# A decode-step kernel: the output sum in four column tiles of one PSUM bank instead of two row groups in two banks

## Chip, core and metric

One core of one Trainium2 chip runs one launch of the kernel. The metric is the device time of a launch in microseconds (us); smaller is better. Beside the timed runs there is one profiled execution, whose trace lists every instruction of the five engines (PE, the TensorE matmul unit, with its weight loads PEld; DVE, the VectorE; ACT, the ScalarE; POOL, the GpSimd; SP, the SyncE, which here only issues transfers) and every transfer.

## The reference

A normalised input of four tokens (one per batch row, D = 576) goes through an attention over the last 2,048 positions of a key and value cache, and through an MLP mixer; both results and the input are summed.

```python
def reference(A_x, A_k_cache, A_v_cache, A_wq, A_wo, B_x, B_w1, B_w2, B_w3, B_w4):
    def _A_ref(x, k_cache, v_cache, wq, wo):          # B=4, Hq=32, Hkv=16, Sk=8192, Dh=128, W=2048
        q = (x @ wq).reshape(B, Sq, Hq, Dh).transpose(0, 2, 1, 3)
        k = jnp.repeat(k_cache[:, :, Sk - W:, :], rep, axis=1)
        v = jnp.repeat(v_cache[:, :, Sk - W:, :], rep, axis=1)
        scores = jnp.einsum("bhqd,bhkd->bhqk", q, k) * (Dh ** -0.5)
        o = jnp.einsum("bhqk,bhkd->bhqd", _softmax(scores, axis=-1), v)
        return o.transpose(0, 2, 1, 3).reshape(B, Sq, Hq * Dh) @ wo
    def _B_ref(x, w1, w2, w3, w4):                    # D=576, F=4608
        ...
        x1 = x + hs
        return x1 + _gelu(_layernorm(x1, axis=-1) @ w3) @ w4
    x = A_x
    xn = _layernorm(x, axis=-1)
    return x + _A_ref(xn, A_k_cache, A_v_cache, A_wq, A_wo) + _B_ref(xn, B_w1, B_w2, B_w3, B_w4)
```

With a sequence of one token the shifted groups that make `hs` are all zero, so `x1` is `xn`, and `w1` and `w2` are not read. What is left to read is two caches of 33.6 MB each and the weights `wq`, `wo`, `w3`, `w4`: 87.17 MB in all.

## The kernel before

**Loads.** All large loads are issued by SP, in program order, into one SBUF tile, `ring` (L113), whose regions are used again and again. An issue waits on SP until the instructions that read the region's former content are done. The order is: `wq` and `w3` (L151 to L153), the key cache in pairs and single tiles of 4 MB (`cache_load`, L126), the first half of `w4` (L509), the value cache in eight tiles, V0 to V7, and at the end 14 rows of the second half of `w4` (L562, `end[0]`), `wo` in two pieces of 23 and 9 rows of 576 columns (L565), and the remaining 3 and 1 rows of `w4` (`end[1]` and `end[2]`).

**Stages.** A prologue normalises the input, makes the transposed copies and runs the first MLP product (L248) and the query product (L267). The key stage turns each key tile with DVE transposes (L321) and multiplies (L330, sixteen times four matmuls of 512 columns in four column tiles for every tile). Then come the exponentials, and the value stage: DVE spreads the probabilities (L402), PE multiplies them by the value tiles (L415). From L516 to L578 the order of PE, ACT and DVE is written out by hand (`tc.manual_schedule`); before that the framework orders the instructions of an engine.

**The output sum.** All products that end in the output, 68 rows in all, are summed in PSUM without being copied out: 36 rows of `w4` (`mlp_out`, L495, with the columns of `gT`, the MLP's activations) and 32 rows of `wo` (L575, with the columns of `onx`, the attention's heads). `acc_matmuls` (L466) takes a weight operand of 4 columns (the four batches) and a row of 576 columns, and issues two matmuls of 288 columns each: the left half goes to partitions 0 to 3 of the bank `ACC`, the right half to partitions 32 to 35 of a second bank `ACC2`. `ACC` is opened early by a matmul with zeros (L215), and the residual `xn + x` is written into it by two DVE copies (L232). `ACC2` is opened inside the value stage after the third value tile (L545 to L547): a matmul with zeros, and a DVE copy of the right half's residual.

**The end.** After V7 the last heads are picked (L441, L439, L449, L454, L458), in between run rows of `w4`; five matmuls with zeros (`idle`, L572) keep PE working; then PE does the 32 rows of `wo` and the rows of `end[1]` and `end[2]`. DVE copies the left half to `fin`, ACT the right half (L582, 4 partitions x 288 each), and ACT issues one output transfer of 4 rows of 1,152 bytes (L583).

Of the kernel before, what the change touches and what calls it, by code (L numbers as in the profile page):

```python
# [11 lines left out]
BF16 = mybir.dt.bfloat16  # L12
F32 = mybir.dt.float32
# [5 lines left out]
def kernel(  # L19
# [19 lines left out]
    nc = tc.nc  # L39
    P = 128  # L40
    B, Sq, D = A_x.shape
# [13 lines left out]
    NF = F // P  # L55
    NFH = NF // 2
    NQ = Hq * Dh
    DC = (D // 2, D // 2)
    NI = 4
    NI1 = NFH - NI * NI  # L60
    NG2 = (NI + 1) * P
# [6 lines left out]
    o2 = out.flatten_outer_dims()  # L68

    def ap_of(t, offset_elems, dims):  # L70
        a = t[:]
        return bass.AP(a.tensor, a.offset + offset_elems, [list(a.ap[0])] + [list(d) for d in dims])
# [10 lines left out]
    const = ctx.enter_context(tc.tile_pool(name="const", bufs=1))  # L83
    small = ctx.enter_context(tc.tile_pool(name="small", bufs=2))
# [4 lines left out]
    ps_s = ctx.enter_context(tc.tile_pool(name="ps_s", bufs=4, space=PSUM))  # L89
# [19 lines left out]
    REST = 4 * TILE  # L109
    RING = max(SLOT[2] + wq_n + w3_n, REST + E0_N)  # L110
    assert wo_n + sum(E1) * D <= 2 * TILE
    LEAD = 16
    ring = ringp.tile([P, LEAD + RING], BF16, tag="ring", name="ring")[:, LEAD:LEAD + RING]  # L113

    def load_run(t, src):
# [28 lines left out]
    XR = wo_n // D  # L144
    NT = Hq * Dh // (P * XR)
# [12 lines left out]
    ident = const.tile([P, P], BF16)  # L158
# [22 lines left out]
    def z_part(n, dt):  # L181
        a = z_at[0]
        z_at[0] += n * (1 if dt is BF16 else 2)
        assert z_at[0] <= ZN
        return Z[:, a:a + n] if dt is BF16 else Zf[:, a // 2:a // 2 + n]
# [10 lines left out]
    def turned(src, count, name):  # L196
        tp = ps_tp.tile([P, count, B], BF16, tag="tp", name=name)
        for k in range(count):
            nc.tensor.transpose(out=tp[:, k, :], in_=src(k), identity=ident[0:B, 0:B])  # L199
        return tp  # L200
# [3 lines left out]
    xn_f, xn_bf, ln2_bf = (z_part(D, dt)[0:B] for dt in (F32, BF16, BF16))  # L204
# [6 lines left out]
    ACC = ps_acc.tile([P, 512], F32)  # L211

    zeros = const.tile([P, 512], BF16)
    nc.vector.memset(zeros[:], 0.0)
    nc.tensor.matmul(out=ACC[:], lhsT=ident[:], rhs=zeros[:], start=True, stop=False, skip_group_check=True)  # L215
    gT = const.tile([P, NF, B], BF16)


    QN = 512
# [8 lines left out]
    l_dup = half_rows(ln2_bf, 0, NS, NO)  # L228
    ln2T = const.tile([P, 2 * NO, B], BF16)
    nc.vector.tensor_tensor(out=xn_f[:], in0=xn_f[:], in1=x_bf[:], op=ALU.add)  # L230
    for q in range(2):
        nc.vector.tensor_copy(out=ACC[32 * q:32 * q + B, 0:DC[q]], in_=xn_f[:, q * DC[0]:q * DC[0] + DC[q]])  # L232
    tpl = turned(lambda k: l_dup[:, k % 2, NO - 1 - k // 2, :], 2 * NO, "tpl")
    nc.vector.tensor_copy(out=ln2T[:], in_=tpl[:])

# [26 lines left out]
    for j in range(-1, KJ):  # L262
        for h in range(2 if j >= 0 else 1):
            k = 2 * j + 1 - h if j >= 0 else 2 * KJ + 1
            for i in range(QI):
                f0 = (j * NQ + WT if j >= 0 else 0) + h * WT + i * QN
                nc.tensor.matmul(out=qp[32 * i:32 * i + 2 * B, :], lhsT=xnT[:, k:k + 2, :].rearrange("p e b -> p (e b)"),  # L267
                                 rhs=wq_t[:, f0:f0 + QN], start=False, stop=False, skip_group_check=True)
# [13 lines left out]
    for y in range(NY):  # L282
        for m in range(HB):
            m2, r = divmod(m, rep)
            nc.tensor.matmul(out=tq[:, :, :, m2, y, r, :],
                             lhsT=q_rows[:, m, y, :, :].rearrange("p g i -> p (g i)"), rhs=rows,
                             start=(y + m == 0), stop=(y == NY - 1 and m == HB - 1), skip_group_check=True)
# [13 lines left out]
    S = []  # L301
# [44 lines left out]
    for g0 in range(2):  # L346
        for mh in range(2):
            nc.gpsimd.tensor_copy(out=ap_of(perm_rows, 16 * g0 + 8 * mh, [[32, B], [2, 4], [1, rep]]),
                                  in_=ap_of(ident, 8 * g0 + 16 * mh, [[rep, B], [32, 4], [1, rep]]))
# [4 lines left out]
                   in_=ap_of(perm_rows, 0, [[PB, 2], [1, rep], [rep, MT]]))  # L354
# [74 lines left out]
                             start=True, stop=True, skip_group_check=True)  # L429
        nc.scalar.copy(out=rd_rows[:], in_=RD[:])  # L430

    onx = const.tile([P, NT, XR, B], BF16)

    def heads_out(bp):
        for j in range(2):
# [17 lines left out]
    def heads_pick(bp, OX):  # L453
        nc.vector.tensor_tensor(out=masked.rearrange("p t b x e -> p (t b) x e"),  # L454
                                in0=OX[:].rearrange("p t b (e x) -> p (t b) x e", x=XR),
                                in1=ap_of(own_d, 0, [[0, NT * 2], [0, XR], [1, ND]]), op=ALU.mult)
        with nc.allow_low_precision(reason="one term of each sum is not zero"):
            nc.vector.tensor_reduce(out=ap_of(onx, 2 * bp, [[XR * B, NT], [1, 2], [B, XR]]),  # L458
                                    in_=masked, op=ALU.add, axis=AX.X)

    ACCS = [ACC]

    def acc_rows(q):
        return slice(32 * q, 32 * q + B)

    def acc_matmuls(lhsT, row):  # L466
        for q in range(2):
            nc.tensor.matmul(out=ACCS[q][acc_rows(q), 0:DC[q]], lhsT=lhsT, rhs=row[:, q * DC[0]:q * DC[0] + DC[q]],  # L468
                             start=False, stop=False, skip_group_check=True)

    def gelu_u():
        nc.vector.scalar_tensor_tensor(out=gu, in0=gx[:], scalar=GA, in1=gx[:], op0=ALU.mult, op1=ALU.mult)
# [3 lines left out]
    def gelu_g():  # L476
        nc.vector.scalar_tensor_tensor(out=gg[:], in0=gu, scalar=1.0, in1=gx[:], op0=ALU.add, op1=ALU.mult)

    def gelu_T():
        GT = ps_tp.tile([P, NF, B], F32, tag="tp", name="GT")  # L480
        for i in range(NI + 1):
            n = NI if i < NI else NI1
            c_step = NI if i < NI else 1
            cols = bass.AP(ident[:].tensor, ident[:].offset, [list(ident[:].ap[0]), [32, n], [B, 2], [1, B]])
            out = ap_of(GT, (i if i < NI else NI * NI) * B, [[c_step * B, n], [NFH * B, 2], [1, B]])
            nc.tensor.matmul(out=out, lhsT=gg[:, i * P:(i + 1) * P], rhs=cols, start=(i == 0), stop=(i == NI),
                             skip_group_check=True)
        nc.scalar.mul(out=gT[:], in_=GT[:], mul=0.5)  # L488

    def load_w4(a, e, i0, n):  # L490
        t = ring[:, a:a + n * D]
# [2 lines left out]

    def mlp_out(t, e, i0, n, a=0, b=None):  # L495
        for i in range(a, n if b is None else b):
            acc_matmuls(gT[:, e * NFH + i0 + i, :], t[:, i, :])


    for n in range(len(K_order)):  # L500
# [16 lines left out]
    with tc.manual_schedule(engines=ENGINES):  # L517
        exponentials(0)
        first = ps_s.tile([P, rep, CK], F32, tag="S", name="first")
        for r in range(rep):  # L520
            pick_rows(0, r, first[:, r, :], 0, 1)
        exponentials(1)
        exponentials(2)
        for r in range(rep):
            nc.scalar.copy(out=CB[:, 0, 0, :, r], in_=first[:, r, :])
        exponentials(3)
        spread_rows(0)
        v_compute(0, 0, CK // 2)
        pick_all(0)
        keep_rows(0, 1, NG)  # L530
        v_compute(0, CK // 2, CK)
        cache_load(v_rows, 4, 1, V_tiles)
        spread_rows(1)
        reciprocals()
        nc.scalar.copy(out=spread, in_=bass.AP(fold[:].tensor, fold[:].offset, [list(fold[:].ap[0]), [1, PB], [0, ND]]))
        for n in range(1, NV):
            if n + 1 < NV:
                spread_rows(n + 1)
            v_compute(n)
            if n == 1:  # L540
                pick_all(1)
                keep_rows(1, 0, NG)
            if n == 2:
                reciprocal_rows()
                ACCS.append(ps_s.tile([P, 512], F32, tag="S", name="ACC2"))  # L545
                nc.tensor.matmul(out=ACCS[1][:], lhsT=ident[:], rhs=zeros[:], start=True, stop=False, skip_group_check=True)  # L546
                nc.vector.tensor_copy(out=ACCS[1][acc_rows(1), 0:DC[1]], in_=ACC[acc_rows(1), 0:DC[1]])  # L547
            if n == 3:
                heads_out(0)
            if n == 4:  # L550
                heads_pick(0, heads_rows(0))
                gelu_u()
            if n == 6:
                gelu_g()
                gelu_T()
                mlp_out(*w4_e0, 0, NFH // 2)
            if n + 4 < NV:
                cache_load(v_rows, n + 4, 1, V_tiles)
            if n == 5:
                wo_t, end, i0 = ring[:, 0:wo_n], [], 0  # L560
                for k, n1 in enumerate(E1):
                    end.append(load_w4(wo_n + i0 * D, 1, i0, n1))  # L562
                    i0 += n1
                    for a, b in ((0, XF * D), (XF * D, wo_n)) if k == 0 else ():
                        load_run(wo_t[:, a:b], flat(A_wo, wo_n)[:, a:b])  # L565
        heads_out(1)
        mlp_out(*w4_e0, NFH // 2, NFH * 2 // 3)
        OX = heads_rows(1)
        mlp_out(*w4_e0, NFH * 2 // 3, NFH)
        heads_pick(1, OX)  # L570
        mlp_out(*end[0])
        idle = ps_s.tile([P, 512], F32, tag="S", name="idle")  # L572
        for i in range(5):
            nc.tensor.matmul(out=idle[:], lhsT=ident[:], rhs=zeros[:], start=(i == 0), stop=(i == 4), skip_group_check=True)
        for x in range(XR):  # L575
            acc_matmuls(onx[:, 0, x, :], wo_t[:, x * D:(x + 1) * D])
        for part in end[1:]:
            mlp_out(*part)  # L578

    fin = const.tile([B, D], out.dtype, name="fin")  # L580
    for q, copy in enumerate((nc.vector.tensor_copy, nc.scalar.copy)):
        copy(out=fin[:, q * DC[0]:q * DC[0] + DC[q]], in_=ACCS[q][acc_rows(q), 0:DC[q]])  # L582
    nc.scalar.dma_start(out=o2, in_=fin[:])  # L583


# [28 lines left out]
```

## Time and profile before

| | |
|---|---|
| median of 3 runs | 210.72 us (210.34 to 210.96) |
| the profiled execution's own time | 210.92 us |
| its span, first to last instruction | 209.1 us |
| mean granted PE clock | 0.755 of full speed |
| busy: PE, DVE, ACT, POOL | 122.2, 128.0, 13.2, 4.3 us |
| PE matmuls, with as many weight loads | 1077 |

The span is what the trace shows; the rest of the execution's 210.92 us, 1.8 us, lies around it. Durations below are those of this one execution, to be held against its own time.

How the rows are read: a row of a timeline is "start, duration, engine, line, operation, written tile <- read tiles, shape, count, and in brackets the idle time of the engine before it and what ended that". An overlapping run of like instructions is merged into one row. A row of the stretches view gives for each engine the busy time and the number of instructions, the granted clock, and the share of time in which the core's 16 DMA engines were busy (a transfer is counted where it began, so a stretch can read a little over 1).

### The profile page before, as it was taken

The page shows a single profiled execution, that of the slowest core. Times are in us where ns is not written, and L with a number is a line of the kernel's source. Part 1 is how long each engine was busy: PE and PEld are TensorE (multiplying, and loading weights), DVE is VectorE, ACT ScalarE, POOL GpSimd, SP SyncE. Part 2 cuts the span into 40 slices and gives each one's busy share as a digit, 9 for nine tenths or more (in the row PEclk, how much of TensorE's full clock was granted, in tenths as well). Part 3 has the DMA queues.
Part 4 walks back from the last instruction along what each step waited for, and adds up shares of the span by engine and source line. Part 5 has one row for each costly group of instructions (what it writes and reads, how often), then busy time and mean ns, then how long its engine had stood idle before and what let it go on. Part 6 is the DMA issues. An engine that isn't in the chain of part 4 may idle for free.

```text
span 209.1 us, 2429 instructions
## 1 busy us (share of the span) xinstructions
PE 122.2 (58%) x1077; PEld 76.3 (36%) x1077; DVE 128.0 (61%) x120; ACT 13.2 (6%) x34; POOL 4.3 (2%) x15
## 2 busy tenths in 40 slices
PE   1318951001543333454333341999999999999994
PEld 0101211000111101111111110678788889878652
DVE  5930021009996999999999937139946578940200
ACT  2000022000000000000000023020210001000000
POOL 2500000000000000000000000000000000000000
PEclk9999997555555555555555555599999999999999
DMA  8989999999997999999999999999799999999991
GB/s 339 397 381 489 514 392 401 414 401 501 476 414 307 476 426 393 432 464 407 427 543 422 404 414 426 401 539 404 338 464 429 407 451 442 401 425 439 446 384 68
DMA packets 3057, 87.31 MB, mean 417 GB/s; under 512 B 348, under 2 KB 488, under 8 KB 744
## 3 DMA queue, kind: packets, MB, share of 16 engines
q1 hardware_dynamic: 3024, 87.16, 97.1%
q8 instruction: 8, 0.13, 0.2%
q10 hardware_dynamic: 24, 0.01, 0.0%
q14 instruction: 1, 0.01, 0.0%
HBM read 87.17 MB, written 0.00 MB: 417 GB/s over the span
## 4 chain that ended last, share of the span: by engine, by line
DMA 26%; PE 23%; DVE 7%; SPq 0%; issue 0%; DVEq 0%
PE O L415 20%; DMA ring<-in_A_v_cache_dram 14%; DMA ring<-in_A_wo_dram 13%; DVE kt L321 6%; PE C L379 2%; PE ACC L468 1%; DVE mx L305 0%; PE OX L449 0%; DVE fin L582 0%; SPq L116 0%; PE RD L428 0%; SPq L492 0%; PE ACC L546 0%; DVEq L321 0%
## 5 line engine op out<-in xcount | busy, mean ns | idle before, releaser
L321 DVE STREAM_TRANSPOSE kt<-ring 128x2048 int32<-128x2048 int32 x32 | 70.7, 2275 | 14.7 <-DMA ring<-in_A_k_cache_dram 14.7
L330 PE MATMUL S<-kt,Z 128*32 128x512 bf16 x256 | 30.4, 622 | 60.3 <-DVE kt L321 60.3
L415 PE MATMUL O<-ring,X 128*128 128x256 bf16 x512 | 59.5, 280 | 4.9 <-DMA ring<-in_A_v_cache_dram 4.8
L415 PEld LDWEIGHTS <-X 128*128 128x128 bf16 x512 | 51.3, 100 | 13.0 <-issue 3.0
L402 DVE TENSOR_TENSOR X<-Z,own 128x1024 int32<-128x1024 int32 x32 | 37.0, 1217 | 11.2 <-ACT Z L389 8.2
L330 PEld LDWEIGHTS <-Z 128*32 128x32 bf16 x256 | 9.9, 127 | 80.0 <-issue 74.7
L248 PE MATMUL G<-ring,ln2T 128*8 128x512 bf16 (+1 forms) x54 | 10.5, 862 | 3.9 <-DMA ring<-in_B_w_dram 3.9
L278 DVE CAST q_rows<-qp 128x256 bf16<-128x256 f32 x4 | 1.5, 418 | 16.7 <-PE qp L267 16.0
L439 DVE TENSOR_SCALAR Z<-O,rd_rows 64x128 f32<-64x128 f32 x2 | 0.7, 357 | 13.5 <-ACT Z L441 13.5
L371 ACT ACTIVATE Z<-S,nb 128x512 bf16<-128x512 f32 x4 | 2.8, 702 | 89.9 <-DVE nb L514 89.9
L248 PEld LDWEIGHTS <-ln2T 128*8 128x8 bf16 x54 | 2.0, 98 | 11.3 <-issue 9.9
L582 DVE CAST fin<-ACC 4x288 bf16<-4x288 f32 x1 | 0.4, 446 | 7.9 <-PE ACC L468 7.9
L468 PE MATMUL ACC<-ring,gT 128*4 128x288 bf16 x72 | 5.1, 286 | 0.4 <-ACT gT L488 0.4
L468 PE MATMUL ACC<-ring,onx 128*4 128x288 bf16 x64 | 4.3, 286 | 0.3 <-DMA ring<-in_A_wo_dram 0.2
L389 ACT CAST Z<-C 128x384 bf16<-128x384 f32 (+1 forms) x4 | 2.7, 663 | 21.6 <-PE C L379 21.5
L379 PEld LDWEIGHTS <-pick 128*128 128x128 bf16 x24 | 2.4, 111 | 4.3 <-issue 2.8
L199 PEld LDWEIGHTS <-Z 4*128 4x128 bf16 x16 | 0.7, 104 | 8.8 <-DVE Z L174 5.0
L305 DVE TENSOR_REDUCE mx<-S 128x1 f32<-128x512 f32 x4 | 2.7, 671 | 2.0 <-PE S L330 2.0
L379 PE MATMUL C<-Z,pick 128*128 128x512 bf16 x16 | 3.8, 379 | 0.0
L468 PEld LDWEIGHTS <-gT 128*4 128x4 bf16 x72 | 3.0, 84 | 1.8 <-ACT gT L488 0.5
L468 PEld LDWEIGHTS <-onx 128*4 128x4 bf16 x64 | 2.9, 84 | 1.9 <-issue 1.0
L547 DVE COPY ACC<-ACC 4x288 f32<-4x288 f32 x1 | 0.5, 462 | 4.7 <-PE ACC L546 4.7
(81 smaller groups left out, 46.7 us busy)
## 6 DMA issues: line engine op xcount, KB each, us to landing
ring<-in_A_k_cache_dram SPq DMA_DIRECT2D x4, 4096.0 KB, 20.5
ring<-in_A_v_cache_dram SPq DMA_DIRECT2D x4, 4096.0 KB, 20.3
ring<-in_B_w_dram SPq DMA_DIRECT2D x1, 5184.0 KB, 15.5
ring<-in_A_wq_dram SPq DMA_DIRECT2D x1, 4096.0 KB, 24.7
ring<-in_A_wo_dram SPq DMA_DIRECT2D x1, 3312.0 KB, 23.6
ring<-in_B_w_dram SPq DMA_DIRECT2D x1, 2592.0 KB, 26.9
ring<-in_B_w_dram SPq DMA_DIRECT2D x1, 2016.0 KB
ring<-in_A_wo_dram SPq DMA_DIRECT2D x1, 1296.0 KB, 26.3
```

Of the source, the lines that this page charges most:

```text
L199: nc.tensor.transpose(out=tp[:, k, :], in_=src(k), identity=ident[0:B, 0:B])
L248: nc.tensor.matmul(out=G_banks[k][32 * c:32 * c + 2 * B, 0:n * P].rearrange("p (i m) -> p i m", m=P), lhsT=ln2T[:, NS - 1 - s:NS + 1 - s, ...
L278: nc.vector.tensor_copy(out=dst, in_=src)
L305: nc.vector.reduce_max(out=mx[:, g:g + 1], in_=S[g][:], axis=AX.X)
L321: nc.vector.transpose(out=ap32(kt[e], c0 * 2 * G, [[2 * G, C2 // 2], [1, 2], [2, G]]), in_=ap32(kn, c0 * 4 * G + e * G, [[4 * G, C2 // 2], ...
L330: nc.tensor.matmul(out=S[kq][c:c + 32, :].rearrange("p (c q l) -> p c q l", q=4, l=2), lhsT=qz[:, bp, m, y, :], rhs=kt[e][:, :, 4 * m:4 * ...
L371: nc.scalar.activation(out=EP[:, g].rearrange("p q (c l) -> p c q l", l=2), in_=S[g][:].rearrange("p (c q l) -> p c q l", q=4, l=2), func= ...
L379: nc.tensor.matmul(out=out, lhsT=pick[:, bp, r, 3 - q:3 - q + P], rhs=EP[:, g0:g1, q, :], start=(q == 0), stop=(q == 3), skip_group_check= ...
L389: nc.scalar.copy(out=CB[:, bp, g0:g1, :, r], in_=CPS[bp, r][:, g0 * CK:g1 * CK].rearrange("p (g c) -> p g c", c=CK))
L402: nc.vector.tensor_tensor(out=ap32(X, a * CX * MT, [[MT, CX], [1, MT]]), in0=bass.AP(s32.tensor, s32.offset, [list(s32.ap[0]), [1, CX], [0 ...
L415: nc.tensor.matmul(out=O_tiles[bp][:], lhsT=X[:, c:c + 2, :].rearrange("p c n -> p (c n)"), rhs=vn[:, c:c + 2, :].rearrange("p c d -> p (c ...
L468: nc.tensor.matmul(out=ACCS[q][acc_rows(q), 0:DC[q]], lhsT=lhsT, rhs=row[:, q * DC[0]:q * DC[0] + DC[q]], start=False, stop=False, skip_gr ...
```

## The change

The sum lies in one bank, in four column tiles: columns 144q to 144q+143 of the output lie on partitions 32q to 32q+31 of `ACC`, columns 0 to 143. Within a tile the four batches lie eight partitions apart (0, 8, 16, 24). Each row is four matmuls of 144 columns with a weight operand of 25 columns. For that `gT` and `onx` hold the four batches of row i at the columns 5i, 5i+8, 5i+16, 5i+24, in zeroed tiles; the 25 columns from 5i on also hold values of other rows, at places that are no multiple of 8, whose products land on partitions that nobody reads. The residual comes in by four fp32 matmuls with a small operand `place` instead of by DVE copies. `ACC2`, its zero matmul and its DVE copy are gone. At the end one ACT copy takes all 128 partitions x 144 to `fin`, and the output transfer takes every eighth partition: 16 rows of 288 bytes. `LEAD` is changed by 352 bytes per partition.

```diff
-    DC = (D // 2, D // 2)
+    DQ = 4
+    DW = D // DQ
+    BS = 32 // B
+    LS = 5
+    LW = BS * (B - 1) + 1
...
-    LEAD = 16
+    LEAD = 192
...
-    gT = const.tile([P, NF, B], BF16)
+    gT = const.tile([P, LS * (NF - 1) + LW], BF16)
+    nc.gpsimd.memset(gT[:], 0.0)
...
-    for q in range(2):
-        nc.vector.tensor_copy(out=ACC[32 * q:32 * q + B, 0:DC[q]], in_=xn_f[:, q * DC[0]:q * DC[0] + DC[q]])
+    place = small.tile([B, LW], F32, tag="place")
+    nc.gpsimd.memset(place[:], 0.0)
+    nc.gpsimd.tensor_copy(out=place[:, 0:LW:BS], in_=ident[0:B, 0:B])
+
+    def acc_matmuls(lhsT, row):
+        for q in range(DQ):
+            nc.tensor.matmul(out=ACC[32 * q:32 * q + LW, 0:DW], lhsT=lhsT, rhs=row[:, q * DW:(q + 1) * DW],
+                             start=False, stop=False, skip_group_check=True)
+
+    acc_matmuls(place[:], xn_f)
...
-    onx = const.tile([P, NT, XR, B], BF16)
+    onx = const.tile([P, LS * (XR - 1) + LW], BF16)
+    nc.gpsimd.memset(onx[:], 0.0)
...
-            nc.vector.tensor_reduce(out=ap_of(onx, 2 * bp, [[XR * B, NT], [1, 2], [B, XR]]),
+            nc.vector.tensor_reduce(out=ap_of(onx, 2 * bp * BS, [[0, NT], [BS, 2], [LS, XR]]),
...
-    def acc_matmuls(lhsT, row):
-        for q in range(2):
-            nc.tensor.matmul(out=ACCS[q][acc_rows(q), 0:DC[q]], lhsT=lhsT, rhs=row[:, q * DC[0]:q * DC[0] + DC[q]],
-                             start=False, stop=False, skip_group_check=True)
+    def row_cols(t, i):
+        return t[:, LS * i:LS * i + LW]
...
-        nc.scalar.mul(out=gT[:], in_=GT[:], mul=0.5)
+        nc.scalar.mul(out=ap_of(gT, 0, [[LS, NF], [BS, B]]), in_=GT[:], mul=0.5)
...
-            acc_matmuls(gT[:, e * NFH + i0 + i, :], t[:, i, :])
+            acc_matmuls(row_cols(gT, e * NFH + i0 + i), t[:, i, :])
...
-                ACCS.append(ps_s.tile([P, 512], F32, tag="S", name="ACC2"))
-                nc.tensor.matmul(out=ACCS[1][:], lhsT=ident[:], rhs=zeros[:], start=True, stop=False, skip_group_check=True)
-                nc.vector.tensor_copy(out=ACCS[1][acc_rows(1), 0:DC[1]], in_=ACC[acc_rows(1), 0:DC[1]])
...
-            acc_matmuls(onx[:, 0, x, :], wo_t[:, x * D:(x + 1) * D])
+            acc_matmuls(row_cols(onx, x), wo_t[:, x * D:(x + 1) * D])
...
-    fin = const.tile([B, D], out.dtype, name="fin")
-    for q, copy in enumerate((nc.vector.tensor_copy, nc.scalar.copy)):
-        copy(out=fin[:, q * DC[0]:q * DC[0] + DC[q]], in_=ACCS[q][acc_rows(q), 0:DC[q]])
-    nc.scalar.dma_start(out=o2, in_=fin[:])
+    fin = const.tile([P, DW], out.dtype, name="fin")
+    nc.scalar.copy(out=fin[:], in_=ACC[:, 0:DW])
+    step = fin[:].ap[0][0]
+    nc.scalar.dma_start(out=o2.rearrange("b (q c) -> q b c", q=DQ),
+                        in_=bass.AP(fin[:].tensor, fin[:].offset, [[BS * step, DQ * B], [1, DW]]))
```

## The prediction, made before the changed kernel was run

> **What bounds the kernel now.** I read the page first, then the same span by stretches, then the issue and landing of the last loads, then the last three microseconds instruction by instruction.
>
> ```profile
> span 209.1 us, 2429 instructions
> PE 122.2 (58%) x1077; PEld 76.3 (36%) x1077; DVE 128.0 (61%) x120; ACT 13.2 (6%) x34; POOL 4.3 (2%) x15
> HBM read 87.17 MB, written 0.00 MB: 417 GB/s over the span
> ```
>
> No engine is busy for two thirds of the span, while 417 GB/s are read over all of it. The stretches show whether the transfers ever pause:
>
> ```profile
> 50.00:100.00 50.00, 20.87 (x176) 6.76 (x176) 48.17 (x23) 0.00 (x0) 0.00 (x0) 0.50 0.98 419
> 100.00:150.00 50.00, 29.56 (x228) 18.90 (x228) 36.70 (x30) 4.57 (x13) 0.00 (x0) 0.64 1.00 432
> 150.00:204.00 54.00, 52.90 (x517) 44.39 (x516) 27.53 (x30) 3.65 (x8) 0.00 (x0) 1.00 0.99 426
> ```
>
> The columns are stretch, length, busy us of PE, PEld, DVE, ACT and POOL, PE clock, DMA share, GB/s. The last two hardly move: the 16 DMA engines are full from the first load to 204, whichever engine is busy beside them. So the loads set the time, and the engines matter in two ways only: if one kept a buffer so long that the queue ran dry, or in what is left after the last load has landed. The first does not happen: a value tile takes 20.3 us from issue to landing where 4 MB at 426 GB/s take 9.8, so about ten microseconds of transfers lie queued at each issue. For the second, the last three loads:
>
> ```profile
> 178.84 0.90 SPq L492 DMA_DIRECT2D ring<-in_B_w_dram  x2
> ...
> ring<-in_B_w_dram SPq DMA_DIRECT2D x1, 432.0 KB, 26.9
> ring<-in_B_w_dram SPq DMA_DIRECT2D x1, 144.0 KB, 26.8
> ```
>
> The two issues at 178.84 and 179.31 (the pair ends at 179.74, the second takes 0.43) are end[1] and end[2], the last four rows of the sum; with 26.9 and 26.8 us to landing they arrive at 205.74 and 206.11. The 9 rows before them arrive with wo's second piece: PE waits for it until 204.72, by the chain of waits, which ends "DMA wo 26.32 from 178.37, PE ACC 1.80 from 204.72, DVE fin 0.43". And now PE and the end:
>
> ```profile
> 205.82 0.66 PE L468 MATMUL ACC<-ring,gT 128*4 128x288 bf16 x8
> 206.15 0.08 PEld L468 LDWEIGHTS <-gT 128*4 128x4 bf16 x1
> 206.51 0.45 DVE L582 CAST fin<-ACC 4x288 bf16<-4x288 f32 x1 [7.93 <-PE ACC L468]
> 206.55 0.39 ACT L582 CAST fin<-ACC 4x288 bf16<-4x288 f32 x1 [10.04 <-PE ACC L468]
> 207.04 0.27 ACTq L583 DMA_DIRECT2D out_dram<-fin  x1
> ```
>
> The reader is to see the second row: the very last weight load began at 206.15, 0.04 after the landing at 206.11, because it stood behind the matmul that waited for the load. The last two matmuls began at 206.20, 122 ns after the pair before (288 columns at 2.4 per ns are 120). So the chain of waits names PE for the last 1.80 us, but PE is late by only 206.20 - 206.15 = 0.05 us; behind that stands the last load. This is what I choose to build on.
>
> **The change part by part.**
>
> *Row pace.* Two matmuls of 288 columns in two column tiles run together: a row takes 122 ns (64 in 4.38 us with one stop). Four of 144 in four tiles would take 61 if they also run together, as the sixteen of L330 do (four of 512 columns in about 427 ns at clock 0.50). They need eight PE instructions per row instead of four. The nearest row for an issue limit is L285: 16 matmuls of 32 columns with 128-column weights in 0.64 us, 25 ns apart in a run; four one after another would be 100 ns a row. It does not matter which: PE must do 12 rows between 204.72 and 206.15, so any pace up to 1.43 / 12 = 119 ns is covered by the last load. The 23 rows of wo's first piece have 204.72 - 201.61 = 3.11 us, 135 ns each. The 0.73 us that 12 rows win at 61 ns become waiting, in front of 204.72, 205.74 and 206.11. Gain: 0.05 us. If the cover were gone it would be 0.05 + 0.7.
>
> *Last matmul.* It ends 0.286 after its start now; 144 columns fewer take 0.06 less. With the four starting together (L330's starts lie within 0.03), the sum ends at 206.15 + 0.01 + 0.23 = 206.39 instead of 206.48, a gain of 0.09 with the 0.05 in it. PE will stand idle more: between 201.15 and 204.57 the 23 rows take 1.4 us instead of 3.2. The granted clock fell to 0.50 at 33.9 us after 3.4 us with 0.64 busy, and did not after 3.4 us with 1.86 busy; 1.4 lies between, nearer to the second. If it falls, the last rows take about 122 ns again and the last matmul some 0.08 more: the gain of 0.09 is gone, no more. I take no fall.
>
> *Copy.* ACT began 0.065 after the matmul's end, took 0.389, DVE ended at 206.96, and the transfer was issued 0.08 later. One ACT copy of 128x144 from PSUM: gT at L488 has just this shape and took 0.290 (128x128 at L257: 0.272). So 206.39 + 0.065 + 0.29 + 0.08 = 206.83 for the issue, against 207.04: 0.21 gained, the 0.09 included.
>
> *Output transfer.* From its issue at 207.04 to SP seeing it landed were 1.29 us, then 0.8 to the span's end. Four packets of 1,152 bytes become 16 of 288; no row of the trace shows such a write. From below: the four landings lay 0.14 apart, which more parallel sources could remove, -0.14. From above: issues of 128 rows took 0.42 to 0.54 against 0.27, +0.26, and sixteen packets in one line at the 29 ns of x_bf's 576-byte ones are 0.46 against the 0.18 that the four take, +0.28; together +0.54. Sixteen rows are far nearer to 4 than to 128, and x_bf's short packets ran side by side: I take +0.05.
> The Trainium skill speaks against the change here: "DMA: Bandwidth & Descriptors", Specifications, puts the smallest transfer for full rate at 512 B, below which the engine reads, modifies and writes. No run here shows such a write yet; with that page's 0.2 us for an access to HBM, an estimate, the transfer would be 0.2 longer and the time 210.7.
>
> *Moved or removed elsewhere.* The four fp32 `place` matmuls and the POOL work (memsets of gT, onx and place, one copy; POOL is busy 4.3 us in all) fall into the prologue, where the first product waits 3.9 us for w3 (G at L248 <- DMA 3.9); PE's transposes queue behind `place`, but DVE loses two copies of 0.45 there. If that cover were gone, it would still lie ahead of the full queue. The ACC2 matmul (0.38) and copy (0.46) at 158.3 leave the value stage, and the 9 rows at 187.57 shrink from 1.27 us to 0.6 to 0.9; but V7 starts at 188.96 on its own landing, so both become waiting there. gT and onx are written with a stride at the same element count: nothing. LEAD makes up for smaller tiles ahead of the ring: nothing.
>
> Sum: -0.21 + 0.05 = -0.16, which I round to -0.2: the profiled execution's span goes from 209.1 to 208.9 and its time, with the 1.8 us around the span unchanged, from 210.92 to 210.7. The median of the runs shown lies 0.20 below that execution, so the forecast for it is **210.5 us**.
>
> **Rivals.**
>
> *PE pays per matmul (slower).* In L468 each matmul costs 61 ns; if that were a price per matmul and not per column, a row would take 244. Then from 197.59 on: 20 rows 4.88, idle 1.08, 36 rows 8.78, to 212.33; the last ends about 212.5 instead of 206.48, less 0.12 for the copy: +5.9, 216.6 us. It decides from 119 ns a row, a price of 30 ns per matmul. For it: 61 in L468 and 109 in L415 are the only long runs. Against it: L285's 25 ns, though these 16 had waited 2.80 us and lay ready, and 120 ns of columns explain the 122. The Trainium skill, "TensorE: Matmul & The Clock Gate", section "Wait — 56ns, not 53.3ns?", knows such a price: about 62 ns per matmul when the sequencer's firmware decodes, none with hardware decoding. The L285 row agrees with the second.
>
> *Instruction loads in the way of the data.* PE's program grows by some 280 instructions, and the instruction queue brought eight packets, 0.13 MB, for PE's 2,154: one or two more. Each puts one of 16 DMA engines behind: at 206.1 the 16 landings of the last load, one for each engine, spread over 1.76 us in the trace's records, seven at the front, eight within 0.26 of the end. One more on a fresh engine joins the late half and costs nothing; on one that is already late it would cost up to 0.9 to 1.6: 211.4 to 212.1.
>
> *A slow output.* More than the bound above: it needs some +0.85 to be seen, 211.4. For it only the short writes; against it that even 0.46 in one line does not reach that.
>
> *The last loads come sooner (faster).* If landings at 205.74 and 206.11 were late for a reason that the change removes, PE's 0.73 would count: -0.16 - 0.7 = 209.8. Against it: 87 MB at full rate, the same bytes in the same order.
>
> **Chances.** A measurement of this kernel can tell about 0.3%, 0.63 us, from no change (the three runs spread that far). The forecast, clock falling or not and output within its bounds: 0.64, between 210.1 and 211.0, all of it within 0.3%, but for a part of 0.04 that the runs' spread puts below 210.1. Sooner loads 0.12. PE's price 0.07, instruction loads 0.10, slow output 0.07; of the instruction loads some 0.03 stays within 0.3%. So faster 0.16, same 0.63, slower 0.21. The range for 8 in 10 goes from 209.8, the sooner loads, to 211.4, the lower end of the instruction loads; outside lie PE's price and the tails.
>
> **What would show it.** Right: rows of four L468 matmuls 61 to 100 ns apart, PE idle before the wo pieces and before the last row, the last matmul starting at the last landing, a copy of 0.29, the span shorter by the copy alone. Wrong: four matmuls of a row starting one after another and no PE idle before 206; the last landing moved from 206.1; the clock at 0.50 in the last rows; more than 1.9 us from the output's issue to its landing.

## The result, and the profile after

| | before | after |
|---|---|---|
| median of 5 runs each | 210.72 us (210.34 to 210.96) | 212.22 us (212.02 to 212.40) |
| ratio | | 1.0073 (95% interval 1.0058 to 1.0087) |
| the profiled execution's time, its span | 210.92, 209.1 us | 212.22, 210.4 us |

The changed kernel is slower by 1.5 us. It lies outside the forecast's range; the two profiled spans differ by 1.3. The page of the changed kernel, its heads and the instruction queue:

```profile
span 210.4 us, 2716 instructions
PE 118.3 (56%) x1220; PEld 74.7 (35%) x1220; DVE 126.8 (60%) x116; ACT 13.6 (6%) x34; POOL 5.1 (2%) x19
q8 instruction: 9, 0.15, 0.2%
HBM read 87.17 MB, written 0.00 MB: 414 GB/s over the span
```

And the same queue's line on the page of before:

```profile
q8 instruction: 8, 0.13, 0.2%
```

PE is busy for 3.9 us less and the kernel is slower: the same bytes take longer. q8 brings instructions, and moved nine packets instead of eight. Next the last two loads, end[1] and end[2], in the view of DMA issues (size of each, us from issue to landing):

```profile
ring<-in_B_w_dram SPq DMA_DIRECT2D x1, 432.0 KB, 28.0
ring<-in_B_w_dram SPq DMA_DIRECT2D x1, 144.0 KB, 29.1
```

They took 26.9 and 26.8 before. Both were issued 1.1 to 1.2 earlier than before; the first landed at 205.69 (205.74 before), the second at 207.26 instead of 206.10. The timeline of the end shows what PE made of that:

```profile
201.55 1.62 PE L242 MATMUL ACC<-ring,onx 128*25 128x144 bf16 x92 [1.38 <-DMA ring<-in_A_wo_dram]
204.65 0.74 PE L242 MATMUL ACC<-ring,onx 128*25 128x144 bf16 x36 [1.48 <-DMA ring<-in_A_wo_dram]
205.73 0.37 PE L242 MATMUL ACC<-ring,gT 128*25 128x144 bf16 x12 [0.34 <-DMA ring<-in_B_w_dram]
207.30 0.24 PE L242 MATMUL ACC<-ring,gT 128*25 128x144 bf16 x4 [1.20 <-DMA ring<-in_B_w_dram]
207.59 0.28 ACT L585 CAST fin<-ACC 128x144 bf16<-128x144 f32 x1 [11.13 <-PE ACC L242]
207.90 0.60 ACTq L587 DMA_DIRECT2D out_dram<-fin  x1
```

PE now waits for each of the last loads it needs (the brackets): 1.38 and 1.48 for the two pieces of wo, 0.34 for end[1], and 1.20 for end[2], in front of the last row. The copy and the issue follow at once. The chain of waits says the same, start and length of each step:

```profile
178.15 29.11 DMA ring<-in_B_w_dram
...
207.30 0.27 PE ACC L242 x4
...
207.59 0.28 ACT fin L585
```

With the landing of the output transfer from the records of transfers (206.10, 207.04, 208.31 and 209.1 before; 207.26, 207.90, 209.61 and 210.4 after), the whole span is accounted for:

| stretch | before | after | difference |
|---|---|---|---|
| to the last load's landing | 206.10 | 207.26 | +1.15 |
| from there to the output's issue | 0.93 | 0.64 | -0.29 |
| from the issue to its landing | 1.27 | 1.71 | +0.44 |
| from there to the span's end | 0.8 | 0.8 | 0 |

So there are two losses to explain, and one small gain of the kind that was forecast (0.29, where the working had 0.21).

**The first loss in the records.** Every load lands in sixteen parts, one for each DMA engine. For end[2], in us before the last of the sixteen:

```
before 206.104: 1.76 1.75 1.74 1.68 1.62 1.56 1.38 | 0.76 | 0.26 0.23 0.19 0.10 0.09 0.08 0.06 0
after  207.255: 3.22 3.17 3.16 3.14 3.07 2.99 2.76 | 2.23 | 1.92 1.72 1.57 1.46 1.39 1.39 1.22 0
```

Before, seven engines are at the front, 1.4 to 1.8 us ahead of the last, eight are late, within 0.3 of the last, and one is in between. After, fifteen engines had landed by 207.255 - 1.218 = 206.04, as before; a single one comes 1.22 later. The late group has seven left, so the one behind is one of the eight that were late already. The ninth instruction packet, 16 KB, ran from 205.227 for 0.975 us. These are all the records of transfers from 205.46 to the output's (start in us, ns, queue, bytes), with the packet ahead of them; the pieces of 4 bytes are completion marks:

```
205.227 975 q8 16384
...
205.482  51 q1 1152
205.529  51 q1 1152
205.576  51 q1 1152
205.623   9 q1 4
206.188 138 q1 1152
206.312  25 q1 4
```

Only as the packet ends (206.20) do a last row's piece and a last completion mark run, 0.69 after all other marks. The records do not name engines, but this is what an engine looks like that still owed its piece when the packet came. The eight packets before had each put one engine back; the number of late engines grows from one at 46.9 us to eight. What the extra PE instructions brought is a packet to an engine that was late already. PE's program grew from 2 x 1077 to 2 x 1220 instructions, and a packet came for about every 256 of them (in the kernel before, 1,790 traced instructions of PE started from the first packet to the eighth, over seven steps).

### The profile page after: what moved, and what is told of

It is laid out like the page before. It is cut to its first block, busy times and chain, and to the rows that moved or that the text cites. A ratio compares the mean times of both kernels' runs of the same rounds, so it can differ in the third digit from the quotient of the medians.

```text
span 210.4 us, 2716 instructions
## 1 busy us (share of the span) xinstructions
PE 118.3 (56%) x1220; PEld 74.7 (35%) x1220; DVE 126.8 (60%) x116; ACT 13.6 (6%) x34; POOL 5.1 (2%) x19
## 4 chain that ended last, share of the span: by engine, by line
DMA 28%; DVE 15%; PE 13%; SPq 1%; issue 0%; ACT 0%; DVEq 0%
DVE kt L334 15%; DMA ring<-in_B_w_dram 14%; DMA ring<-in_A_v_cache_dram 14%; PE O L428 12%; DVE mx L318 1%; SPq L120 0%; SPq L499 0%; PE OX L463 0%; PE RD L441 0%; ACT fin L585 0%; PE ACC L242 0%; DVEq L334 0%
## 5 line engine op out<-in xcount | busy, mean ns | idle before, releaser
L428 PE MATMUL O<-ring,X 128*128 128x256 bf16 x512 | 58.5, 277 | 6.0 <-DMA ring<-in_A_v_cache_dram 6.0
L242 PE MATMUL ACC<-ring,gT 128*25 128x144 bf16 x144 | 3.2, 227 | 2.4 <-DMA ring<-in_B_w_dram 1.5
L242 PE MATMUL ACC<-ring,onx 128*25 128x144 bf16 x128 | 2.4, 226 | 2.9 <-DMA ring<-in_A_wo_dram 2.9
L242 PEld LDWEIGHTS <-gT 128*25 128x25 bf16 x144 | 2.4, 94 | 3.1 <-issue 2.1
L242 PEld LDWEIGHTS <-onx 128*25 128x25 bf16 x128 | 2.1, 94 | 3.4 <-issue 3.4
L280 PE MATMUL qp<-ring,xnT 128*8 128x512 bf16 x36 | 3.1, 403 | 0.0
L203 PE MATMUL tpx<-ident,Z 4*128 4x4 bf16 x6 | 0.5, 173 | 4.5 <-DVE Z L178 4.5
```

The lines of the kernel that those rows point to most:

```text
L242: nc.tensor.matmul(out=ACC[32 * q:32 * q + LW, 0:DW], lhsT=lhsT, rhs=row[:, q * DW:(q + 1) * DW], start=False, stop=False, skip_group_chec ...
L428: nc.tensor.matmul(out=O_tiles[bp][:], lhsT=X[:, c:c + 2, :].rearrange("p c n -> p (c n)"), rhs=vn[:, c:c + 2, :].rearrange("p c d -> p (c ...
```

## The experiments

Theory of the first loss: the ninth instruction packet falls on an engine that is already late, and what counts is the number of PE's instructions, whatever they compute. Rival: the new instructions, shapes or the new wait of PE hold up the loads. Theory of the second loss: the output transfer is dear for its form; rivals below.

### The first loss: instruction packets

**a_less64**, the changed kernel with 64 PE instructions fewer: 32 of the 256 score matmuls of the key stage are left out, so part of the scores is missing:

```diff
                 y = 2 * e + t
+                if n < 4 and y == 3:
+                    continue
                 for m in range(NM):
```

> The changed kernel with 64 PE instructions less, taken from the key stage: 32 of its 256 score matmuls (the last of four groups, in the first four key tiles) are left out, where PE waits for DVE anyway. Instruction-load theory: the ninth 16 KB packet of PE instructions, which began at 205.23 and ran on an engine that still owed its part of end[2], is no longer needed, so eight packets remain, the last load lands near 206.1 instead of 207.26 and the time is about 211.1 (212.22 - 1.15). Rival, the denser four-tile matmuls themselves hold up the last transfers: nothing changes, 212.2.

210.79 us (210.61 to 211.12), ratio to the kernel before 1.0010 (1.0001 to 1.0019), where the changed kernel has 1.0073: of the 1.5 us 1.3 are gone, with the whole change in place. A ninth packet is still there, at 205.387, and the record next to it shows why it does no harm: a completion mark started at 205.381, so that engine had done its last piece. The end in its timeline:

```profile
205.87 0.10 PEld L242 LDWEIGHTS <-gT 128*25 128x25 bf16 x3 [0.25 <-issue]
206.16 0.28 ACT L587 CAST fin<-ACC 128x144 bf16<-128x144 f32 x1 [10.00 <-PE ACC L242]
206.47 0.61 ACTq L589 DMA_DIRECT2D out_dram<-fin  x1
```

The last load landed at 205.83 and its weights follow in 0.04; the issue itself remains long (0.61), so the two losses are separate. The packet's time alone does not decide: in l64_sp (below) the ninth came at 205.140, earlier than the changed kernel's at 205.227, but 6 ns after a completion mark, and end[2] landed at 205.93 with no engine behind (the next 0.03 earlier).

**b_more192**, the kernel before, with nothing of the change, and 96 tiny matmuls with zeros (192 PE instructions) in the prologue:

```diff
     nc.tensor.matmul(out=qp[:], lhsT=ident[:], rhs=zeros[:], start=True, stop=False, skip_group_check=True)
+    for _ in range(96):
+        nc.tensor.matmul(out=qp[:, 0:4], lhsT=ident[:], rhs=zeros[:, 0:4], start=False, stop=False, skip_group_check=True)
```

> The kernel before with the same 96 tiny zero matmuls in the prologue and nothing else. Its eighth instruction packet came at 201.19 with 148 traced PE instructions left, so 192 more should bring a ninth within the last 90 instructions, near 204 to 206. Instruction-load theory: the last landing moves from 206.1 to about 207 and the time from 210.7 to about 211.8. Rival, the four-tile matmuls are the cause: 210.7, as this kernel has none.

211.96 us (211.87 to 212.27), ratio 1.0067 (1.0052 to 1.0082). Its page and its timeline:

```profile
q8 instruction: 9, 0.15, 0.3%
```

```profile
206.77 0.66 PE L470 MATMUL ACC<-ring,gT 128*4 128x288 bf16 x8 [1.25 <-DMA ring<-in_B_w_dram]
207.98 0.27 ACTq L585 DMA_DIRECT2D out_dram<-fin  x1
```

The ninth packet came at 204.673, the last load landed at 207.06, one engine 1.45 behind all others, and the old matmuls of 288 columns now wait 1.25 for it. The issue is as short as ever. This is the first loss without any of the change, by work in the prologue alone: the rival falls.

**a_more192**, the changed kernel with the same 96 matmuls, so that the ninth packet comes early and a tenth follows.

> The changed kernel with 192 PE instructions more, 96 tiny matmuls that add zeros in the prologue, where PE waits; so each instruction packet comes 192 instructions earlier, the ninth near 201 to 203 instead of 205.2. Instruction-load theory, first form (the packet hurts an engine wherever it falls, because the queue never lets it catch up, and the ninth falls on an engine that already had one): still late, landing near 207.3 and 212.2. Second form (it hurts only when it comes so late that it meets an engine that is already the last): landing near 206.1 to 206.4 and about 211.1 to 211.4. Rival, the denser matmuls: 212.2.

211.97 us, ratio 1.0066 (1.0051 to 1.0081). The ninth came at 200.957; the second piece of wo landed at 205.52 with one engine 1.11 behind, and end[2] at 206.95, still 1.11 behind. The tenth, at 205.18, added nothing. So a ninth that comes 4 us earlier costs about the same, and the delay stays.

**b_more448**, the kernel before with 224 tiny matmuls, to bring the ninth packet into the value stage and a tenth before the end.

> The kernel before with 224 tiny zero matmuls in the prologue (448 PE instructions more), so the ninth packet of PE instructions comes near 190 and a tenth near 203. If the packets go round eight engines, the ninth and the tenth fall on the two that had the first and the second: in the last load two engines land 1.1 to 1.6 after the other late ones, which stay six, and the time is about 212 again, as with one such packet. If they go round sixteen, the ninth and tenth fall on fresh engines: ten late engines close together, and 210.6.

211.79 us (211.43 to 211.87), ratio 1.0049 (1.0033 to 1.0065). The ninth, at 190.903, put one engine 1.31 behind in the landing of end[0], and it still was at the end (1.27 in end[2], which landed at 206.92). The tenth, at 205.216, started 6 ns after a completion mark and did nothing: one engine behind, not two. What two packets on late engines cost has not been seen.

The landings of these kernels side by side, from the records:

| kernel | the packet that came before its engine was done | end[2] landed | the next engine, earlier by |
|---|---|---|---|
| before | none | 206.10 | 0.06 |
| changed | 205.227 | 207.26 | 1.22 |
| a_less64 | none | 205.83 | 0.13 |
| b_more192 | 204.673 | 207.06 | 1.45 |
| a_more192 | 200.957 | 206.95 | 1.11 |
| b_more448 | 190.903 | 206.92 | 1.27 |
| a_warm (below) | 204.673 | 206.91 | 1.34 |

**b_probe** and **a_probe**, both kernels with four tiny loads of 8, 4, 2 and 1 rows queued behind the last load, whose landings were to show which engines are late:

```diff
+                for k in (8, 4, 2, 1):
+                    nc.sync.dma_start(out=probe[0:k, 64 * k:64 * k + 64], in_=A_wo[0:k, 0:64])
```

> The kernel before, with four tiny loads queued by SP behind the last load, of 8, 4, 2 and 1 rows of 128 bytes, to a tile that nobody reads. A transfer of n rows runs on n engines here (the output's four rows made four landings), so their landings show which of the 16 engines are late at the end. If the instruction packets go round a fixed set of eight engines, the eight landings of the first probe are all late (within 0.6 of the end) or all early (1.4 to 1.8 before it). If they go round all 16, the eight show a mixture. The time stays that of before.

> The changed kernel with the same four tiny loads behind the last load. If the ninth packet falls on the engine that had the first of a round of eight, the engine that lands some 1.2 us after all others is one of those eight. If the round is of 16, it is an engine that had none, and then the extra landing time is not explained by two packets on one engine. Time near 212.2 either way.

One run each: 211.58 and 211.64 us, beside 210.50 for the kernel before; the four loads and the waits for them at the end cost time themselves. The eight parts of b_probe's 8-row load landed on five engines of the front, the half-late one and two late ones, so the late eight are neither all among the engines that it uses nor all outside them. The expectation had read such a mixture as packets that go round all sixteen; but it fits as well a fixed eight of which this load uses only some, so the probe decides nothing. In a_probe the ninth packet came at 205.555, after its engine was done, no engine stood out, and a_probe is 0.6 below the changed kernel in spite of the added loads. In five of five kernels the ninth packet, where it came before its engine was done, met a late one and never a fresh one. That the packets go round a fixed set of eight engines would give this; it is not shown directly.

### The second loss: the output transfer

The theories were: a first use of the form costs (a_warm); the three-level address and the number of DMA engines (l64_flat); the issuing engine (l64_sp); one transfer instead of several (l64_out4); the short pieces (b_short); the distance of the source partitions (b_stride). The l64 kernels are built on a_less64, to be free of the first loss.

**a_warm**: the changed kernel, with an early load in the output's form into `fin`.

```diff
+    nc.scalar.dma_start(out=bass.AP(fin[:].tensor, fin[:].offset, [[BS * fin[:].ap[0][0], DQ * B], [1, DW]]),
+                        in_=x2.rearrange("b (q c) -> q b c", q=DQ))
```

> The changed kernel with one more transfer at the very start: ACT loads 16 rows of 288 bytes in the three-level form of the output transfer into the tile that the output later leaves from. If the output transfer's 0.60 us of issue (0.27 before) and its 1.24 us to the first packet (0.76 before) are the price of a first use of this form, the issue falls to about 0.3 and the time by about 0.3 to 0.45, to 211.8. If they are the price of the form and the 16 rows themselves, nothing changes: 212.2.

212.01 us, ratio 1.0064 (1.0047 to 1.0081); the issue takes 0.59 as in the changed kernel's 0.60. It is no price of a first use.

**l64_flat**, a two-level address (the rows of the output come out permuted), and **l64_sp**, issued by SP:

```diff
-    nc.scalar.dma_start(out=o2.rearrange("b (q c) -> q b c", q=DQ),
+    nc.scalar.dma_start(out=o2.rearrange("b (q c) -> (b q) c", q=DQ),
```

```diff
-    nc.scalar.dma_start(out=o2.rearrange("b (q c) -> q b c", q=DQ),
+    nc.sync.dma_start(out=o2.rearrange("b (q c) -> q b c", q=DQ),
```

> The changed kernel with 64 PE instructions less (32 score matmuls left out), and the 16 output rows of 288 bytes written one after the other in the order of the partitions, a two-level pattern, so the output's rows are permuted. If the output transfer's extra 0.33 us of issue and 0.48 us to the first packet come from the three-level pattern (or from the four-way split that its first level allows), the issue falls to about 0.3 and the time by 0.3 to 0.45 below 210.79, to about 210.4. If they come from the 16 short rows: no change, 210.8.

> The changed kernel with 64 PE instructions less (32 score matmuls left out), and the same three-level output transfer issued by SP instead of ACT. If the price belongs to ACT as the issuer: the issue falls to about 0.3 and the time to about 210.4. If it belongs to the form: 210.8, or 0.05 more for the step from ACT to SP.

Issue 0.58 and 0.69, landing 1.75 and 1.77 after the issue's start, against 1.73 in a_less64; ratios 1.0011 for both (0.9999 to 1.0023). Nothing gained. In l64_flat the rows landed on sixteen engines, in the others on four, and the time is the same.

**l64_out4**: four transfers, one for each column tile, two by ACT and two by SP.

```diff
+    for q in range(DQ):
+        (nc.scalar, nc.sync)[q % 2].dma_start(
+            out=o2[:, q * DW:(q + 1) * DW],
+            in_=bass.AP(fin[:].tensor, fin[:].offset + 32 * q * step, [[BS * step, B], [1, DW]]))
```

> The changed kernel with 64 PE instructions less (32 score matmuls left out), and the output in four two-level transfers of 4 rows of 288 bytes, two issued by ACT and two by SP. If the three-level form is the price: two issues of about 0.27 on each queue, 0.54 in all, the last landing about 1.3 after the second issue's start: 0.1 to 0.2 below 210.79, near 210.65. If short rows are the price, each issue is dearer: 211 or more.

212.24 us, ratio 1.0074 (1.0055 to 1.0093), the worst form:

```profile
206.70 1.54 SPq L590 DMA_DIRECT2D out_dram<-fin  x2
206.70 1.30 ACTq L590 DMA_DIRECT2D out_dram<-fin  x2
```

Four rows each, and every issue takes 0.60 to 0.75, as long as one of sixteen rows. The price is paid by each transfer, not by the row; the last landed 2.81 after the first issue.

**b_stride**: the kernel before, with four rows of 1,152 bytes still, but read from partitions 0, 8, 16 and 24 (three of the four rows are zeros). **b_short**: the kernel before, with four pieces of 288 bytes from partitions 0 to 3 (three quarters of the output are not written).

```diff
-    nc.scalar.dma_start(out=o2, in_=fin[:])
+    nc.scalar.dma_start(out=o2, in_=bass.AP(fin[:].tensor, fin[:].offset, [[8 * fin[:].ap[0][0], B], [1, D]]))
```

```diff
-    nc.scalar.dma_start(out=o2, in_=fin[:])
+    nc.scalar.dma_start(out=o2[:, 0:D // 4], in_=fin[:, 0:D // 4])
```

> The kernel before, whose output transfer reads its 4 rows of 1,152 bytes from partitions 0, 8, 16 and 24 of a wider tile instead of 0 to 3 (three of the rows are zeros instead of results). If the distance between the source partitions is what made the output transfer dear (0.27 us of issue and 1.27 to the landing before; 0.60 and 1.71 after): issue near 0.6, landing 1.6 to 1.75 after its start, span 0.3 to 0.45 longer than before. If it is the short pieces: 0.27 and 1.27, as before.

> The kernel before, whose output transfer writes only the first quarter of each row, 4 pieces of 288 bytes from partitions 0 to 3 (three quarters of the output are not written). If short pieces are what made the output transfer dear: issue near 0.6 and 1.6 or more to the landing. If it is the distance between the partitions: issue 0.27, landing 1.27 or a little less.

One run each; the last lines of their timelines, b_stride first:

```profile
206.54 0.67 ACTq L584 DMA_DIRECT2D out_dram<-fin  x1
```

```profile
206.48 0.27 ACTq L583 DMA_DIRECT2D out_dram<-fin  x1
```

b_stride landed 1.77 after the issue's start, b_short 1.16; the kernel before has 0.27 and 1.27, the changed one 0.60 and 1.71. The distance of the source partitions alone brings the whole loss, 0.50 here; short pieces bring none. Only a distance of eight was run, so what two or four would cost is not known. The Trainium skill's limit, "DMA: Bandwidth & Descriptors", Specifications, of 512 bytes below which an engine reads, modifies and writes, is not seen in this transfer: 288 bytes landed 0.11 sooner than 1,152.

**l64_adj**: as l64_out4, but the batches on adjacent partitions.

```diff
-    BS = 32 // B
-    LS = 5
+    BS = 1
+    LS = B
...
-    LEAD = 192
+    LEAD = 416
...
+    for q in range(DQ):
+        (nc.scalar, nc.sync)[q % 2].dma_start(out=o2[:, q * DW:(q + 1) * DW], in_=fin[32 * q:32 * q + B, :])
```

> The changed kernel with 64 PE instructions less (32 score matmuls left out), the four batches on adjacent partitions of each column tile instead of eight apart, and the output in four transfers of 4 rows of 288 bytes from adjacent partitions, two issued by ACT and two by SP. If the distance of the partitions was the price: each issue about 0.27 (0.60 to 0.75 with the distance), the last landing about 1.5 after the first issue, and with PE and copy 0.29 earlier than before the time is at or just below the kernel before, ratio 0.999 to 1.0005. If not: issues of 0.6, ratio near 1.007 as with the same four transfers from partitions eight apart.

211.0 us, ratio 1.0018 (1.0008 to 1.0029):

```profile
206.90 0.66 SPq L590 DMA_DIRECT2D out_dram<-fin  x2
206.90 0.62 ACTq L590 DMA_DIRECT2D out_dram<-fin  x2
```

Two issues now take 0.66 and 0.62 together (0.34, 0.27, 0.31, 0.27 singly), where they took 1.54 and 1.30: distance confirmed, 1.2 us of l64_out4 gone. But the four landings follow each other by 0.18, the last 1.72 after the first issue, so four cheap transfers take as long as one dear one. And the span ended 1.07 after the last landing, where it ends 0.83 after it with one output transfer (before, changed, a_less64). The 0.999 to 1.0005 of the expectation was missed by these two.

### Two versions that leave nothing out

**a_q3**: three column tiles of 192 columns, one ACT copy, one transfer of 12 rows. **a_q2**: two tiles of 288, adjacent batches, one ACT copy of 36 partitions, two transfers of four rows.

```diff
-    DQ = 4
+    DQ = 3
...
-    LEAD = 192
+    LEAD = 144
```

```diff
-    DQ = 4
+    DQ = 2
...
-    BS = 32 // B
-    LS = 5
+    BS = 1
+    LS = B
```

> The changed kernel with three column tiles of 192 columns instead of four of 144 (12 rows of 384 bytes in the output): the same design with about 140 PE instructions less, nothing left out. Instruction-load theory: the ninth packet is asked for too late to meet the last load or not at all, the last load lands near 206, and the time is near that of the kernel with 64 score instructions less, 210.8. Rival, one bank with more than two column tiles is what costs: some way between 210.5 and 212.2, near 211.6.

> A version meant to keep what helps: one bank, two column tiles of 288, batches on adjacent partitions, so as many PE instructions for the sum as before and only eight packets before the last load; one ACT copy of 36 partitions x 288; two output transfers of 4 rows of 576 bytes, by ACT and SP at once. Nothing is left out. ACT alone ends its copy about 0.07 before DVE did and shorter rows land about 0.05 sooner: 0.1 below the kernel before, ratio 0.9990 to 1.0005. If one of the two terms was read wrongly: 1.001 or more.

211.11 us (ratio 1.0021, 1.0011 to 1.0032) and 211.08 us (1.0025, 1.0012 to 1.0037). Both lose the first loss: end[2] lands at 206.14 and 206.16. In a_q3 the distant partitions stay, the issue takes 0.81 and lands after 1.90. In a_q2 the last lines are

```profile
206.57 0.39 ACT L585 CAST fin<-ACC 36x288 bf16<-36x288 f32 x1 [9.86 <-PE ACC L242]
206.99 0.33 SPq L588 DMA_DIRECT2D out_dram<-fin  x1
207.00 0.27 ACTq L588 DMA_DIRECT2D out_dram<-fin  x1
```

From the landing to the issue it takes 0.83 instead of the 0.93 of before, but the later of the two transfers lands 1.43 after its issue instead of 1.27. These two differences make +0.06. The last load landed 0.06 later than before, and the span ended 0.93 after the last landing instead of 0.83: together the 0.22 by which its profiled span is longer (209.36 against 209.14). The medians differ by 0.46, as the profiled execution of before lay above its median. The expectation had counted neither the second transfer's later landing nor the longer end. No version was faster than the kernel before.

## Why the prediction was wrong, step by step

**What bounds the kernel: right.** The loads set the time, and PE's win became waiting: 1.38, 1.48 and 0.34 in the brackets of its rows, where before it was mostly busy. The loads came no sooner for it, which answers the faster rival: end[1] landed at 205.69 against 205.74, and fifteen engines of end[2] by 206.04 against 206.10.

**Row pace: right.** The 23 rows of wo's first piece, 92 matmuls, took 1.62 us in all with the last one's 0.23: 62 ns for four matmuls of 144 columns, against the 61 estimated. The rival of a price per matmul, 61 ns each, falls with that; the clock did not fall either: it was granted in full from 204 to 206.2 (1.00), and the last matmul took 0.23.

**Last matmul, copy, issue: right, and a little better.** The last matmuls began 0.04 after the landing (0.10 before), the copy took 0.28 (0.29 estimated), and the stretch from landing to issue lost 0.29, of which 0.21 were forecast. ACT's issue came 0.03 after its own copy, not 0.08.

**Moved work: right.** The prologue and ACC2's removal left no mark on the end: with the first loss taken away by a_less64, the last load lands at 205.83, no later than in the kernel before.

**The step that failed: the last landing.** The sum took the landing at 206.1 as given, since the loads' bytes and order were unchanged. The prediction had the mechanism among its rivals, with a chance of 0.10 ("One more on a fresh engine joins the late half and costs nothing; on one that is already late it would cost up to 0.9 to 1.6: 211.4 to 212.1"). The second half of this sentence is what happened, at +1.15. The fresh engine, which made the first half the default, was never met by a ninth packet in any of the five kernels. The packets were counted rightly ("one or two more"), and the eight late engines were seen; what was not done is to hold the one against the other. Eight packets had made eight late engines, so no packet had yet met an engine twice, and which one the ninth would meet could not be read from the trace: an even chance would have been fairer than the default. That 212.22 lies so near the 212.1 of this rival is partly chance: the landing alone brings 1.15, and 0.39 more came from the output, for another reason.

**The term that was mis-sized: the output transfer**, +0.05 taken, within bounds of -0.14 to +0.54, and +0.44 measured. Short pieces, the reason that was feared, cost nothing in b_short. "Sixteen rows are far nearer to 4 than to 128" chose the number of rows as the measure. It is neither rows nor bytes: four rows from partitions eight apart issue in 0.67 (b_stride), sixteen in 0.60, four from adjacent ones in 0.27.

**The range** ended at 211.4, the lower end of one rival taken alone. Both losses came together: the working's 210.7 for the profiled execution, +1.15 for the landing, +0.39 for the output and -0.08 for the front, makes 212.16, and it was 212.22. That the medians differ by 1.5 and not by the spans' 1.3 comes from the profiled execution of before, which lay 0.20 above its median, while that of after lay on its own.

**What stays open:** which engine each instruction packet goes to, and by what rule; why a packet of 0.97 us leaves its engine 1.1 to 1.5 behind the next one; why distant source partitions are dearer.

## What to carry to other kernels

Where the DMA queues never run dry, instructions are traffic too: count the packets of the instruction queue against the late engines in the landing of the last load before adding instructions, even cheap ones in a prologue, since here 192 more PE instructions cost the unchanged kernel 0.67% and 64 fewer gave the changed one back almost all it had lost. A layout that saves a copy at the end has to be weighed with the transfer that reads it: keep the source partitions of a last small transfer adjacent, and in one transfer. A stage that waits for loads gives nothing back for faster compute, whatever its share of busy time.

## What the runs showed of the hardware

- An instruction packet of 16 KB took 0.9 to 1.1 us, and the engine it met stayed behind for the rest of the span: b_more448's was 1.31 behind at 194.5 and 1.27 at 206.9.
- In the changed kernel the piece behind the packet took 138 ns instead of 51, its mark 25 instead of 9, and the landing was seen 0.94 after the mark's start, where 0.41 lie between the last of the other marks (205.623) and the last of the other landings (206.04).
- A transfer of four rows from partitions eight apart: issue 0.60 to 0.75, landing 1.72 (the first of l64_out4) and 1.77 (b_stride) after its start; from adjacent partitions 0.27 to 0.34, and 1.16 to 1.27 where it was alone or the first. The landings of sixteen rows lay at 1.71 to 1.77, whatever the levels of the address, the issuing engine and the number of engines that the pieces landed on.
- The span ended 0.83 after the last landing with one output transfer (0.94 in a_warm, which has one load more), 0.93 with two (a_q2) and 1.07 with four (l64_out4, l64_adj).
- Four column tiles of 144 columns ran together at 62 ns for all four, 15.5 ns per matmul with its weight load.
